# A transformer block on one core: a later x tile, other scale loads, a touch of the modulation rows, and other PSUM banks

## The chip, the cores and the metric

The kernel runs on one core of one Trainium2 chip. Its time is the device time of one execution in microseconds (us). It is given as the median over runs, and one further execution was taken with the hardware profiler. TensorE is called PE below, its weight loads PEld, VectorE DVE, ScalarE ACT, GpSimd POOL and SyncE SP.

## What is computed

This is a diffusion transformer block. A vector c gives six rows of modulation, two of which scale and shift the normalised x before attention; a third gates the attention's result; the other three do the same for the MLP. B = 2, N = 256, D = 1152, two heads of 576, F = 4608, all in bfloat16.

```python
mod = (_silu(c) @ w_mod).reshape(B, 6, 1, D)
shift_a, scale_a, gate_a, shift_m, scale_m, gate_m = [mod[:, i] for i in range(6)]
h = _layernorm(x, axis=-1) * (1 + scale_a) + shift_a
qkv = (h @ wqkv).reshape(B, N, 3, H, Dh)
...
attn = _softmax(jnp.einsum('bqhd,bkhd->bhqk', q, k) * Dh ** (-0.5), axis=-1)
a = jnp.einsum('bhqk,bkhd->bqhd', attn, v).reshape(B, N, D) @ wo
x = x + gate_a * a
h2 = _layernorm(x, axis=-1) * (1 + scale_m) + shift_m
m = _gelu(h2 @ w_fc1) @ w_fc2
return x + gate_m * m
```

## The kernel before

The 512 rows of x are four tiles of 128 (t = 0 to 3; tiles 0 and 1 are batch 0), and D is nine slices of 128 (kt = 0 to 8). All matrices stay in bfloat16; sums are in PSUM, eight banks of 512 float32 columns.

*Order.* A small planner (class `Sched`) records every operation as a unit with a cost and what it reads and writes, and derives the waits. PE and SP run their units in the order in which the program records them. DVE and ACT begin with lists written by hand (`S.first`); after these, and on POOL from the start, the planner takes the ready unit with the longest path behind it. Nearly all records carry a helper's line: every matmul is L693, every PE transpose L696, every DMA L674, PSUM copies on ACT L688 and on DVE L690.

*Head.* ACT's queue loads c, SP's queue loads x as two halves (`ld_x0`, `ld_x1`, two tiles each), then columns 0 to 639 of the scale matrix in three parts of three kt each (`ld_sc0_0`, `_3`, `_6`), then K's weights `ld_wk0` to `ld_wk4`, the other scale columns (`ld_sc5_*`), and so on. POOL makes the identity (`ones` L715, `ident` L716), which PE needs for everything. PE begins with filler matmuls of 512 columns on the identity (`warm_a`, then after the transpose of c, `c_T`, `warm_b` and so on). silu(c) is made by ACT and DVE (L729 to L731). Normalisation takes its sums on DVE for tiles 1 and 2 (`bn_stats`, L738) and on ACT for tiles 0 and 3 (L746, L747), POOL takes the root (`rstd`, L742 and L751), and DVE writes the normalised tile `xn_t` (L760). PE transposes it into PSUM (`xn_T(t)`), and 45 matmuls of two columns (`sca_kt`, `mod_kt`) give the scale for kt 0 to 4 in bank 7.

DVE adds 1 (`sc1a`, L799), and `hk(kt, b)` (L808 on DVE, L806 on ACT) multiplies the transposed slice in PSUM by it; `xn_T_copy` saves slices 5 to 8 in SBUF for later. Then K begins: `k_pair(kts, i, b)` adds slices kts to two of K's output tiles for batch b. For batch 0 it goes kt by kt over four pairs, with `xn_T(2)` after kt 1 and `xn_T(3)` after kt 2; then comes batch 1. In between, `scb` makes the scale for kt 5 to 8 as rows (36 matmuls, four in the array at a time), a DVE transpose (`scb_T`, L870) and an addition (L872) turn it into columns, and K goes on with kt 5.

*Middle and end.* Shift, Q, softmax, V and the attention's product follow. In `wo_tile(t)` PE makes three pieces of 384 columns, DVE multiplies each by the gate row (`wo_t1`, L1114), POOL adds x (L1115), and DVE and ACT normalise (L738, L1119, L1120). `xn2_T(t)` transposes the result into banks 7 and 6, from where DVE (L1135) and ACT (L1138) write the scaled and shifted slices. The accumulators of these pieces and of the MLP's tiles go around over six banks (`acc`). The first `F0` = 8 tiles of the MLP's first matrix are computed as two halves of 256 rows, the others over all 512. The second matrix (`fc2`) goes tile by tile in pieces of 384 columns; for each, DVE multiplies (L1232) and adds (L1233), and SP stores. The last piece is cut into 224, 96 and 64 columns.

Of the kernel before, what the change touches and what calls it, by code (L numbers as in the profile page):

```python
# [506 lines left out]
CH = 384  # L507
NCH = 3
F0 = 8
KC = 5  # L510
# [33 lines left out]
def build_kernel(nc, x, c, wqkv, wo, w_mod, w_fc1, w_fc2, out):  # L544
# [5 lines left out]
    with (  # L550
# [148 lines left out]
        dma(CSB[0:18, :], c.rearrange("b (k p) -> (b k) p", p=P), 18 * 256, "ld_c", eng="act")  # L699
        for b in range(2):  # L700
            dma(X[:, 2 * b:2 * b + 2, :], xv[b], 2 * P * D * 2, "ld_x%d" % b)
        for (ka, kb) in ((0, KC), (KC, KT)):
            w = (kb - ka) * P
            for k0 in range(0, KT, 3):
                dma(WSC[:, k0:k0 + 3, ka * P:kb * P], wmod_v[:, k0:k0 + 3, D + ka * P:D + kb * P], 3 * P * w * 2,
                    "ld_sc%d_%d" % (ka, k0), run=w * 2)
            for kt in range(ka, kb):
                dma(WK[:, kt, :], wqkv_v[:, kt, D:2 * D], P * D * 2, "ld_wk%d" % kt, run=2304)
        for k0 in range(0, KT, 3):
            dma(WSH[:, k0:k0 + 3, :], wmod_v[:, k0:k0 + 3, 0:D], 3 * P * D * 2, "ld_sh%d" % k0, run=2304)  # L710
# [8 lines left out]

        S.op("pool", 100, lambda e: e.memset(NHALF, -0.5), writes=[NHALF], name="nhalf")  # L720

        dve(600, lambda e: e.memset(Q4B, 0.0), [], [Q4B], "zq4b")
        for i in range(2):
            S.unit("pe", 430.0, "warm_a%d" % i)
            mm(ps32(5), IDENT, Q4B, True, True)
# [27 lines left out]
        for t in range(4):  # L753
            xt, xn, mv, rs = X[:, t, :], XN[:, t, :], MV[:, t, :], RSTD[:, t:t + 1]
            if t in (1, 2):
                ln_stats_dve(xt, [X[:, t, i * CH:(i + 1) * CH] for i in range(NCH)], BN[:, t, :], mv, rs, "ln1_%d" % t)
            else:
                ln_stats_act(xt, xn, mv, SUMS[:, t:t + 1], rs, "ln1_%d" % t)
            m = MV[:, t, 0:1]
            dve(c_dve_fast(D), lambda e, xt=xt, xn=xn, m=m, rs=rs: e.tensor_scalar(out=xn, in0=xt, scalar1=m, scalar2=rs,  # L760
                                                                                 op0=ALU.subtract, op1=ALU.mult),
                [xt, m, rs], [xn], "xn_%d" % t)


        XB = [(4, 5, 6), (6, 4, 5)]

        def xn_T(t):
            b = t // 2
            S.unit("pe", KT * c_mm(128), "xnT_%d" % t)
            for kt in range(KT):  # L770
                tr(ps16(XB[b][kt // 4], (kt % 4) * 256 + (t % 2) * 128, 128), XN[:, t, kt * 128:(kt + 1) * 128], IDENT)

        def xn_T_copy(b, k0, k1, eng):
            src = ps16(XB[b][k0 // 4], (k0 % 4) * 256, (k1 - k0) * 256).rearrange("p (k t) -> p k t", k=k1 - k0)
            copy_on(eng, HX[:, k0:k1, b * 256:(b + 1) * 256], src, (k1 - k0) * 256, True, "xnT_cp%d_%d" % (b, k0))
# [6 lines left out]
        def mod_kt(W, kt, col0, name, fs=(0, 9)):  # L782
            S.unit("pe", (fs[1] - fs[0]) * 27.0, name)
            for f in range(*fs):
                mm(ps32(7, col0 + f * 2, 2), W[:, kt, f * 128:(f + 1) * 128], ST[:, kt:18:9], kt == 0 and f == fs[0], kt == KT - 1,
                   skip_group_check=True)
# [10 lines left out]
        def sc1a(ka, kb):  # L797
            m, o = ps32(7, 2 * ka, 2 * (kb - ka)), SC1A[:, 2 * ka:2 * kb]
            dve(170, lambda e: e.tensor_scalar(out=o, in0=m, scalar1=1.0, scalar2=None, op0=ALU.add), [m], [o], "sc1a_%d" % ka)  # L799


        def hk(kt, b, eng="dve"):
            dst, s1 = HK[:, kt, b * 256:(b + 1) * 256], SC1A[:, kt * 2 + b:kt * 2 + b + 1]
            src = ps16(XB[b][kt // 4], (kt % 4) * 256, 256) if kt < KC else HX[:, kt, b * 256:(b + 1) * 256]
            if eng == "act":
                act(c_act(256, 1), lambda e: e.activation(out=dst, in_=src, func=ACTF.Copy, scale=s1), [src, s1], [dst], "hk_%d_%d" % (kt, b))  # L806
                return
            dve(256 if kt < KC else 200, lambda e: e.tensor_scalar(out=dst, in0=src, scalar1=s1, scalar2=None, op0=ALU.mult),  # L808
                [src, s1], [dst], "hk_%d_%d" % (kt, b))
# [7 lines left out]
        KB = [(0, 1, 2, 3), (5, 4, 6)]  # L817
# [18 lines left out]
        warm(15, "b")  # L836
        xn_T(1)
        for kt in range(0, 3):
            mod_kt(WSC, kt, 0, "sca_%d" % kt, (0, KC))
        warm(1, "c")  # L840
        xn_T(0)
        for kt in range(3, 6):
            mod_kt(WSC, kt, 0, "sca_%d" % kt, (0, KC))
        warm(2, "d")
        for kt in range(6, 9):
            mod_kt(WSC, kt, 0, "sca_%d" % kt, (0, KC))
        warm(3, "e")
        sc1a(0, KC)
        for kt in range(KC):
            hk(kt, 0, "act" if kt in (2, 4) else "dve")  # L850
        xn_T_copy(0, 8, 9, "act")
        xn_T_copy(0, 5, 8, "act")
        for kt in range(KC):
            for i in range(4):
                k_pair((kt,), i, 0)
            if kt == 1:
                xn_T(2)
            if kt == 2:
                xn_T(3)
                xn_T_copy(1, 8, 9, "act")  # L860
                xn_T_copy(1, 5, 8, "act")
        for kt in range(KC):
            hk(kt, 1, "act" if kt == 2 else "dve")
        k_pair(range(KC), 0, 1)
        S.unit("pe", KT * 4 * 27.0, "scb")
        for kt in range(KT):
            quad_mm(6, WSC[:, kt, :], KC, KT, kt)
        n = 32 * (KT - KC)
        sct, scr = ps32(6, 0, n), MT[:, 0:n]
# [6 lines left out]
        k_pair(range(KC), 1, 1)  # L876
        k_pair(range(KC), 2, 1)
# [34 lines left out]
        for kt in range(KT):  # L912
            for b in range(2):
# [5 lines left out]
                else:  # L919
# [174 lines left out]
        acc = [2, 3, 4, 5, 0, 1]  # L1094
# [29 lines left out]
        def xn2_T(t):  # L1124
# [3 lines left out]
            slot = [ps16(7, kt * 128, 128) if kt < 4 else ps16(6, (kt - 4) * 128, 128) for kt in range(KT)]  # L1128
# [161 lines left out]
```

## Time and profile before

| | |
|---|---|
| median of 3 runs | 245.28 us (244.84 to 245.52) |
| profiled execution: time, span | 245.29 us, 243.5 us |
| PE busy | 238.5 us (98%) in 1721 instructions |
| DVE, ACT, POOL busy | 117.0, 67.0, 22.4 us |
| DMA | 51.57 MB, 212 GB/s over the span, some 390 GB/s up to about 70 us |
| granted TensorE clock | 0.999 |

The span runs from the first to the last instruction of the profiled execution; its time has 1.8 us more around it. In a line of the timeline stand the start, the time from the first to the last of the merged instructions, engine, line, operation, output and input, the count, and in brackets how long the engine had been idle before it and what ended that. A matmul's record covers its way through the array, so matmuls overlap, and their pace is read from one start to the next. "DMA to landing" runs from an issue to the last of its 16 completions.

### The profile page before, as it was taken

Reading aid. Unit: us, or ns where it says so; the run is one execution under the profiler, and the core shown is the slowest. Engines: PE = TensorE matmul, PEld = TensorE weight load, DVE = VectorE, ACT = ScalarE, POOL = GpSimd, SP = SyncE. Lnnn points to the kernel's source line nnn. Section 1 sums busy time; section 2 is a strip of 40 time slices with the busy share of each in tenths; the row PEclk is TensorE's granted clock in tenths of the full one; section 3 lists DMA queues with packets and bytes.
Section 4 is the critical chain, followed back from the end, with each engine's and each line's share of the span. In section 5 each row is a group of like instructions: output and inputs, shape, how many; then the busy total and the mean of one; then the engine's idle time right before and its main releaser. Section 6 shows DMA issues by size and latency. Waiting matters only on the chain.

```text
span 243.5 us, 4013 instructions
## 1 busy us (share of the span) xinstructions
PE 238.5 (98%) x1721; PEld 145.9 (60%) x1731; DVE 117.0 (48%) x227; ACT 67.0 (27%) x137; POOL 22.4 (9%) x40
## 2 busy tenths in 40 slices
PE   7999999999999999999999999999999999999995
PEld 2587844466667666888444444444565656566675
DVE  3644359798892689779999500000022221111112
ACT  5630340435614206973223332222000000000000
POOL 1400000000023275500000110000000000000000
PEclk9999999999999999999999999999999999999999
DMA  6999999999995999979943499100000000000000
GB/s 240 361 377 392 391 385 388 405 415 404 387 340 156 351 389 392 391 239 397 338 145 87 167 271 398 57 0 3 0 16 19 16 16 16 19 16 17 31 19 16
DMA packets 30139, 51.57 MB, mean 212 GB/s; under 512 B 1707, under 2 KB 16939, under 8 KB 30123
## 3 DMA queue, kind: packets, MB, share of 16 engines
q1 hardware_dynamic: 29584, 50.14, 57.5%
q0 software_dynamic: 512, 1.19, 1.6%
q8 instruction: 13, 0.21, 0.4%
q14 instruction: 3, 0.02, 0.0%
q10 hardware_dynamic: 27, 0.00, 0.0%
HBM read 50.14 MB, written 1.19 MB: 211 GB/s over the span
## 4 chain that ended last, share of the span: by engine, by line
PE 97%; ACT 1%; issue 0%; DVE 0%; POOL 0%; POOLq 0%
PE psum L693 94%; PE psum L696 2%; ACT arena L1138 1%; ACT arena L1120 1%; DVE arena L808 0%; POOL arena L716 0%; DVE arena L1232 0%; DVE arena L1233 0%; POOL arena L715 0%; DVE arena L799 0%; POOL arena L1022 0%; POOL arena L720 0%; POOLq L1275 0%
## 5 line engine op out<-in xcount | busy, mean ns | idle before, releaser
L693 PE MATMUL psum<-arena 128*128 128x384 bf16 (+9 forms) x1632 | 235.3, 312 | 2.3 <-POOL arena L716 1.5
L693 PEld LDWEIGHTS psum<-arena 128*128 128x128 bf16 (+1 forms) x1642 | 140.5, 97 | 92.5 <-issue 5.2
L1232 DVE TENSOR_TENSOR arena<-psum,arena 128x384 f32<-128x384 f32 (+3 forms) x14 | 7.0, 500 | 89.4 <-PE psum L693 89.4
L1148 ACT ACTIVATE arena<-psum 128x512 bf16<-128x512 f32 (+1 forms) x44 | 22.5, 522 | 42.6 <-PE psum L693 42.6
L688 ACT ACTIVATE arena<-psum 128x512 bf16<-128x512 f32 (+6 forms) x37 | 18.9, 539 | 37.9 <-PE psum L693 37.9
L1049 DVE SCALAR_TENSOR_TENSOR arena<-arena 128x1152 f32<-128x1152 bf16 x16 | 21.3, 1409 | 0.0
L1020 DVE SCALAR_TENSOR_TENSOR arena<-arena 128x896 f32<-128x896 bf16 x16 | 17.6, 1145 | 0.0
L690 DVE CAST arena<-psum 128x512 bf16<-128x512 f32 (+1 forms) x12 | 7.7, 646 | 12.1 <-PE psum L693 12.0
L674 POOL DMA_DIRECT2D dit_scratch<-arena x6 | 3.6, 605 | 95.7 <-ACT arena L688 58.1
L1115 POOL TENSOR_TENSOR arena<-arena 128x384 f32<-128x384 f32 x12 | 10.9, 912 | 11.3 <-DVE arena L1114 10.2
L738 DVE BATCH_NORM_STATS2 arena<-arena 128x6 f32<-128x384 f32 (+1 forms) x18 | 9.5, 549 | 1.5 <-DMA arena<-in_x_dram 0.9
L1120 ACT ACTIVATE arena<-arena 128x1152 bf16<-128x1152 f32 x4 | 5.4, 1353 | 9.5 <-DVE arena L1119 9.5
L1114 DVE TENSOR_TENSOR arena<-psum,arena 128x384 f32<-128x384 f32 x12 | 6.5, 546 | 2.7 <-PE psum L693 1.3
L696 PEld LDWEIGHTS psum<-arena 128*128 128x128 bf16 (+1 forms) x89 | 6.0, 98 | 2.4 <-DMA arena<-in_c_dram 0.8
L696 PE MATMUL psum<-arena 128*128 128x128 bf16 (+1 forms) x89 | 7.3, 219 | 0.1
L1233 DVE TENSOR_TENSOR arena<-arena 128x384 bf16<-128x384 f32 (+3 forms) x14 | 7.0, 502 | 0.5
L1138 ACT ACTIVATE arena<-psum,arena 128x128 bf16<-128x128 bf16 x16 | 6.1, 459 | 3.2 <-PE psum L696 2.5
L1135 DVE TENSOR_SCALAR arena<-psum,arena 128x128 bf16<-128x128 bf16 x20 | 5.5, 336 | 1.9 <-PE psum L696 1.8
L808 DVE TENSOR_SCALAR arena<-psum,arena 128x256 bf16<-128x256 bf16 x7 | 2.4, 349 | 3.6 <-PE psum L696 2.3
L742 POOL TENSOR_TENSOR arena<-arena 128x1 f32<-128x1 f32 x6 | 3.3, 553 | 5.9 <-DVE arena L741 5.9
L964 ACT ACTIVATE arena<-psum,arena 128x256 bf16<-128x256 f32 x8 | 3.7, 470 | 0.0
L917 ACT ACTIVATE arena<-arena 128x256 bf16<-128x256 bf16 x6 | 2.5, 495 | 3.3 <-DVE arena L911 3.3
(57 smaller groups left out, 53.2 us busy)
## 6 DMA issues: line engine op xcount, KB each, us to landing
arena<-in_w_fc_dram SPq DMA_DIRECT2D x9, 1152.0 KB, 7.2
arena<-in_w_fc_dram SPq DMA_DIRECT2D x4, 2592.0 KB, 18.0
arena<-in_w_mod_dram SPq DMA_DIRECT2D x3, 1920.0 KB, 20.4
arena<-in_wqkv_dram SPq DMA_DIRECT2D x18, 288.0 KB, 9.7
arena<-in_w_mod_dram SPq DMA_DIRECT2D x3, 864.0 KB, 12.4
arena<-in_wqkv_dram SPq DMA_DIRECT2D x1, 2592.0 KB, 16.1
arena<-in_wo_dram SPq DMA_DIRECT2D x1, 2592.0 KB, 26.2
arena<-in_w_mod_dram SPq DMA_DIRECT2D x1, 2592.0 KB, 17.9
```

Of the source, the lines that this page charges most:

```text
L688: act(c_act(n), lambda e: e.activation(out=dst, in_=src, func=ACTF.Copy), [src], [dst], name)
L690: dve(c_dve_psum16(n) if psum16 else c_dve_psum32(n), lambda e: e.tensor_copy(dst, src), [src], [dst], name)
L693: S.instr(lambda e: e.matmul(o, lhsT=l, rhs=r, start=st, stop=sp, **kw), reads=[l, r], writes=[o])
L696: S.instr(lambda e: e.transpose(o, i_, idn), reads=[i_, idn], writes=[o])
L738: dve(550, lambda e, s=s, o=o: e.bn_stats(out=o, in_=s), [s], [o], "bn_%s_%d" % (tag, ci))
L1020: dve(150 + FG * 1.1, lambda e, o=o, w=w, s1=s1: e.scalar_tensor_tensor(out=o, in0=w, scalar=s1, in1=o, op0=ALU.mult, op1=ALU.add), [w, s1 ...
L1049: u = dve(1300, lambda e, o=o, w=w, s1=s1: e.scalar_tensor_tensor(out=o, in0=w, scalar=s1, in1=o, op0=ALU.mult, op1=ALU.add), [w, s1, o], ...
L1115: S.op("pool", 930, lambda e, xs=xs, x1c=x1c: e.tensor_tensor(out=x1c, in0=x1c, in1=xs, op=ALU.add), reads=[x1c, xs], writes=[x1c], name=" ...
L1120: act(1344, lambda e: e.activation(out=xn2, in_=x1, func=ACTF.Identity, scale=rs, bias=nm), [x1, rs, nm], [xn2], "xn2_%d" % t)
L1138: act(440, lambda e, o=o, dst=dst, s1=s1, s2=s2: e.activation(out=dst, in_=o, func=ACTF.Identity, scale=s1, bias=s2), [o, s1, s2], [dst], ...
L1148: act(c_act(ntok), lambda e: e.activation(out=dst, in_=o, func=ACTF.Gelu_apprx_tanh), [o], [dst], "gelu_%d_%d" % (f, tok0))
L1232: dve(c_dve_psum32(w), lambda e, o=o, gm=gm, t1=t1: e.tensor_tensor(out=t1, in0=o, in1=gm, op=ALU.mult), [o, gm], [t1], "fc2_t1_%d_%d" % ( ...
```

## The change

- Loads: ACT's queue begins with a read of 64 bytes from every ninth row of w_mod (128 rows) into space that is used only later (`touch`), and c moves to POOL's queue. x comes as tiles 0 and 1 together, then tile 2, and tile 3 only after `ld_wk1`. The first scale columns come in parts of 2, 3, 3 and 1 kt.
- PE's head: five `warm_a` and ten `warm_b` fillers instead of two and fifteen; two scale slices before `xn_T(1)`, three between it and `xn_T(0)`, four after it, and two fillers then. A scale matmul streams 64 columns (silu(c) repeated 32 times) instead of 2, into 64 columns of bank 7, of which `sc1a` reads two.
- Normalisation: tile 2 takes its sums on ACT, tile 3 on DVE. The first slice of batch 0 is copied to SBUF before it is scaled.
- K: `xn_T(3)` comes after the first two pairs of kt 4, batch 1's slices lie in the banks by odd and even kt, batch 1 adds them in the order 0, 2, 1, 4, 3, its second pair comes ahead of `scb` instead of after it, and `scb` goes to bank 7.
- Later: four accumulator banks until the second halves of the MLP's first tiles and six after; `xn2_T` of odd t in banks 1 and 0; F0 = 9; the last piece in 304 and 80 columns.

```diff
@@ -506,7 +506,7 @@
 NCH = 3
-F0 = 8
+F0 = 9
 KC = 5
...
@@ -696,16 +696,18 @@
-        dma(CSB[0:18, :], c.rearrange("b (k p) -> (b k) p", p=P), 18 * 256, "ld_c", eng="act")
-        for b in range(2):
-            dma(X[:, 2 * b:2 * b + 2, :], xv[b], 2 * P * D * 2, "ld_x%d" % b)
-        for (ka, kb) in ((0, KC), (KC, KT)):
+        dma(sb(O_PT, 64), w_mod.rearrange("(p k) f -> p k f", k=KT)[:, 0, D:D + 32], P * 64, "touch", eng="act")
+        dma(X[:, 0:2, :], xv[0], 2 * P * D * 2, "ld_x0")
+        dma(X[:, 2, :], xv[1][:, 0, :], P * D * 2, "ld_x2", run=2304)
+        for (ka, kb, cuts) in ((0, KC, (0, 2, 5, 8, 9)), (KC, KT, (0, 3, 6, 9))):
             w = (kb - ka) * P
-            for k0 in range(0, KT, 3):
-                dma(WSC[:, k0:k0 + 3, ka * P:kb * P], wmod_v[:, k0:k0 + 3, D + ka * P:D + kb * P], 3 * P * w * 2,
+            for k0, k1 in zip(cuts, cuts[1:]):
+                dma(WSC[:, k0:k1, ka * P:kb * P], wmod_v[:, k0:k1, D + ka * P:D + kb * P], (k1 - k0) * P * w * 2,
                     "ld_sc%d_%d" % (ka, k0), run=w * 2)
...
                 dma(WK[:, kt, :], wqkv_v[:, kt, D:2 * D], P * D * 2, "ld_wk%d" % kt, run=2304)
+                if kt == 1:
+                    dma(X[:, 3, :], xv[1][:, 1, :], P * D * 2, "ld_x3", run=2304)
         for k0 in range(0, KT, 3):
...
@@ -717,12 +719,13 @@
+        dma(CSB[0:18, :], c.rearrange("b (k p) -> (b k) p", p=P), 18 * 256, "ld_c", eng="pool")
         S.op("pool", 100, lambda e: e.memset(NHALF, -0.5), writes=[NHALF], name="nhalf")
...
         dve(600, lambda e: e.memset(Q4B, 0.0), [], [Q4B], "zq4b")
-        for i in range(2):
+        for i in range(5):
             S.unit("pe", 430.0, "warm_a%d" % i)
-            mm(ps32(5), IDENT, Q4B, True, True)
+            mm(ps32(7), IDENT, Q4B, True, True)
         CT_PS = ps16(7, 0, 18)
...
@@ -752,7 +755,7 @@
             xt, xn, mv, rs = X[:, t, :], XN[:, t, :], MV[:, t, :], RSTD[:, t:t + 1]
-            if t in (1, 2):
+            if t % 2 == 1:
                 ln_stats_dve(xt, [X[:, t, i * CH:(i + 1) * CH] for i in range(NCH)], BN[:, t, :], mv, rs, "ln1_%d" % t)
...
@@ -762,17 +765,24 @@
-        XB = [(4, 5, 6), (6, 4, 5)]
+        def xt_ps(b, kt, n=1):
+            if b == 0:
+                return (4, 5, 6)[kt // 4], (kt % 4) * 256
+            return (5, 0) if kt == 8 else ((6, 4)[kt % 2], kt // 2 * 256)
...
             for kt in range(KT):
-                tr(ps16(XB[b][kt // 4], (kt % 4) * 256 + (t % 2) * 128, 128), XN[:, t, kt * 128:(kt + 1) * 128], IDENT)
-
-        def xn_T_copy(b, k0, k1, eng):
-            src = ps16(XB[b][k0 // 4], (k0 % 4) * 256, (k1 - k0) * 256).rearrange("p (k t) -> p k t", k=k1 - k0)
-            copy_on(eng, HX[:, k0:k1, b * 256:(b + 1) * 256], src, (k1 - k0) * 256, True, "xnT_cp%d_%d" % (b, k0))
+                bank, c0 = xt_ps(b, kt)
+                tr(ps16(bank, c0 + (t % 2) * 128, 128), XN[:, t, kt * 128:(kt + 1) * 128], IDENT)
+
+        def xn_T_copy(b, kts, eng):
+            bank, c0 = xt_ps(b, kts[0])
+            n = len(kts)
+            src = ps16(bank, c0, n * 256).rearrange("p (k t) -> p k t", k=n)
+            st = kts[1] - kts[0] if n > 1 else 1
+            copy_on(eng, HX[:, kts[0]:kts[-1] + 1:st, b * 256:(b + 1) * 256], src, n * 256, True, "xnT_cp%d_%d" % (b, kts[0]))
...
@@ -781,8 +791,9 @@
             S.unit("pe", (fs[1] - fs[0]) * 27.0, name)
+            sv = ST[:, kt:18:9].unsqueeze(1).broadcast_to([P, 32, 2])
             for f in range(*fs):
-                mm(ps32(7, col0 + f * 2, 2), W[:, kt, f * 128:(f + 1) * 128], ST[:, kt:18:9], kt == 0 and f == fs[0], kt == KT - 1,
+                mm(ps32(7, f * 64, 64).rearrange("p (n b) -> p n b", b=2), W[:, kt, f * 128:(f + 1) * 128], sv, kt == 0 and f == fs[0], kt == KT - 1,
                    skip_group_check=True)
...
@@ -795,13 +806,15 @@
         def sc1a(ka, kb):
-            m, o = ps32(7, 2 * ka, 2 * (kb - ka)), SC1A[:, 2 * ka:2 * kb]
+            m = ps32(7, 64 * ka, 64 * (kb - ka)).rearrange("p (f n) -> p f n", n=64)[:, :, 0:2]
+            o = SC1A.rearrange("p (k b) -> p k b", b=2)[:, ka:kb, :]
             dve(170, lambda e: e.tensor_scalar(out=o, in0=m, scalar1=1.0, scalar2=None, op0=ALU.add), [m], [o], "sc1a_%d" % ka)
...
             dst, s1 = HK[:, kt, b * 256:(b + 1) * 256], SC1A[:, kt * 2 + b:kt * 2 + b + 1]
-            src = ps16(XB[b][kt // 4], (kt % 4) * 256, 256) if kt < KC else HX[:, kt, b * 256:(b + 1) * 256]
+            bank, c0 = xt_ps(b, kt)
+            src = ps16(bank, c0, 256) if kt < KC and kt + b > 0 else HX[:, kt, b * 256:(b + 1) * 256]
             if eng == "act":
...
@@ -814,7 +827,7 @@
-        KB = [(0, 1, 2, 3), (5, 4, 6)]
+        KB = [(0, 1, 2, 3), (5, 6, 4)]
         ev_rr = [0]
...
@@ -833,48 +846,49 @@
-        warm(15, "b")
+        warm(10, "b")
+        for kt in range(0, 2):
+            mod_kt(WSC, kt, 0, "sca_%d" % kt, (0, KC))
         xn_T(1)
-        for kt in range(0, 3):
+        for kt in range(2, 5):
             mod_kt(WSC, kt, 0, "sca_%d" % kt, (0, KC))
-        warm(1, "c")
         xn_T(0)
-        for kt in range(3, 6):
+        for kt in range(5, 9):
             mod_kt(WSC, kt, 0, "sca_%d" % kt, (0, KC))
-        warm(2, "d")
-        for kt in range(6, 9):
-            mod_kt(WSC, kt, 0, "sca_%d" % kt, (0, KC))
-        warm(3, "e")
+        warm(2, "e")
+        xn_T_copy(0, (0,), "dve")
         sc1a(0, KC)
         for kt in range(KC):
-            hk(kt, 0, "act" if kt in (2, 4) else "dve")
-        xn_T_copy(0, 8, 9, "act")
-        xn_T_copy(0, 5, 8, "act")
+            hk(kt, 0, "act" if kt == 4 else "dve")
+        xn_T_copy(0, (8,), "act")
+        xn_T_copy(0, (5, 6, 7), "act")
         for kt in range(KC):
-            for i in range(4):
+            for i in range(2 if kt == KC - 1 else 4):
                 k_pair((kt,), i, 0)
...
                 xn_T(2)
-            if kt == 2:
-                xn_T(3)
-                xn_T_copy(1, 8, 9, "act")
-                xn_T_copy(1, 5, 8, "act")
+        xn_T(3)
+        k_pair((KC - 1,), 2, 0)
+        k_pair((KC - 1,), 3, 0)
+        xn_T_copy(1, (8,), "act")
+        xn_T_copy(1, (5, 7), "act")
+        xn_T_copy(1, (6,), "dve")
         for kt in range(KC):
-            hk(kt, 1, "act" if kt == 2 else "dve")
-        k_pair(range(KC), 0, 1)
+            hk(kt, 1, "act" if kt % 2 else "dve")
+        k_pair((0, 2, 1, 4, 3), 0, 1)
+        k_pair((0, 2, 1, 4, 3), 1, 1)
         S.unit("pe", KT * 4 * 27.0, "scb")
         for kt in range(KT):
-            quad_mm(6, WSC[:, kt, :], KC, KT, kt)
+            quad_mm(7, WSC[:, kt, :], KC, KT, kt)
         n = 32 * (KT - KC)
-        sct, scr = ps32(6, 0, n), MT[:, 0:n]
+        sct, scr = ps32(7, 0, n), MT[:, 0:n]
         dve(c_dve_psum32(n), lambda e: e.transpose(scr, sct), [sct], [scr], "scb_T")
...
                 hk(kt, b)
-        k_pair(range(KC), 1, 1)
-        k_pair(range(KC), 2, 1)
+        k_pair((0, 2, 1, 4, 3), 2, 1)
         for kt in range(KT):
...
@@ -924,11 +938,11 @@
         S.first = {
-            "dve": ["zq4b", "c_half", "c_silu", "bn_ln1_1_0", "bn_ln1_1_1", "bn_ln1_1_2", "aggr_ln1_1", "veps_ln1_1", "bn_ln1_2_0", "nvar_ln1_0", "veps_ln1_0",
-                    "xn_1", "xn_0", "bn_ln1_2_1", "bn_ln1_2_2", "aggr_ln1_2", "veps_ln1_2", "nvar_ln1_3", "veps_ln1_3",
-                    "sc1a_0", "hk_0_0", "xn_2", "hk_1_0", "xn_3", "hk_3_0", "hk_0_1", "hk_1_1", "hk_3_1", "hk_4_1", "scb_T", "sc1a_5"],
-            "act": ["ld_c", "c_tanh", "sq_ln1_0", "sum_ln1_0", "sq_ln1_3", "sum_ln1_3", "xnT_cp0_8", "xnT_cp0_5", "hk_2_0", "hk_4_0",
-                    "hk_2_1", "xnT_cp1_8", "xnT_cp1_5"],
+            "dve": ["zq4b", "c_half", "c_silu", "bn_ln1_1_0", "bn_ln1_1_1", "bn_ln1_1_2", "aggr_ln1_1", "veps_ln1_1", "nvar_ln1_0", "veps_ln1_0",
+                    "xn_1", "xn_0", "nvar_ln1_2", "veps_ln1_2", "xnT_cp0_0", "sc1a_0", "hk_0_0", "hk_1_0", "hk_2_0", "hk_3_0", "xn_2",
+                    "bn_ln1_3_0", "bn_ln1_3_1", "bn_ln1_3_2", "aggr_ln1_3", "veps_ln1_3", "xn_3", "hk_0_1", "hk_2_1", "hk_4_1", "xnT_cp1_6", "scb_T", "sc1a_5"],
+            "act": ["touch", "c_tanh", "sq_ln1_0", "sum_ln1_0", "sq_ln1_2", "sum_ln1_2", "xnT_cp0_8", "xnT_cp0_5", "hk_4_0",
+                    "xnT_cp1_8", "hk_1_1", "hk_3_1", "xnT_cp1_5"],
         }
...
@@ -1091,7 +1105,7 @@
-        acc = [2, 3, 4, 5, 0, 1]
+        acc = [2, 3, 4, 5]
         acc_rr = [0]
...
@@ -1125,7 +1139,8 @@
             S.unit("pe", KT * c_mm(128), "xn2T_%d" % t)
-            slot = [ps16(7, kt * 128, 128) if kt < 4 else ps16(6, (kt - 4) * 128, 128) for kt in range(KT)]
+            hi, lo = ((7, 6), (1, 0))[t % 2]
+            slot = [ps16(hi, kt * 128, 128) if kt < 4 else ps16(lo, (kt - 4) * 128, 128) for kt in range(KT)]
             for kt in range(KT):
...
@@ -1206,6 +1221,9 @@
         mlp_gate(last_h2T[0])
+        k = acc_rr[0] % 4
+        acc[:] = [0, 1] + acc[k:] + acc[:k]
+        acc_rr[0] = 0
         for f in range(F0):
...
@@ -1220,7 +1238,7 @@
             if t == 3:
-                pieces = [(0, CH), (CH, 2 * CH), (2 * CH, 3 * CH - 160), (3 * CH - 160, 3 * CH - 64), (3 * CH - 64, 3 * CH)]
+                pieces = [(0, CH), (CH, 2 * CH), (2 * CH, 3 * CH - 80), (3 * CH - 80, 3 * CH)]
             for (c0, c1) in pieces:
...
```

## The prediction

> **What bounds the kernel now.** I read the busy times and the chain of waits first.
>
> ```profile
> PE 238.5 (98%) x1721; PEld 145.9 (60%) x1731; DVE 117.0 (48%) x227; ACT 67.0 (27%) x137; POOL 22.4 (9%) x40
> ...
> PE 97%; ACT 1%; issue 0%; DVE 0%; POOL 0%; POOLq 0%
> ```
>
> TensorE (PE) is busy for 238.5 of 243.5 us and carries 97% of the chain. So the time is PE's work plus PE's holes, and a change pays only if K's first matmul starts sooner, a hole closes, or the tail shrinks. Then the timeline of the first 13 us.
>
> ```profile
> 1.15 0.28 POOL L716 TENSOR_SCALAR_AFFINE_SELECT arena<-arena 128x128 bf16<-128x128 bf16 x1
> ...
> 1.49 1.03 PE L693 MATMUL psum<-arena 128*128 128x512 bf16 x2 [1.49 <-POOL arena L716]
> ...
> 2.45 0.10 PEld L696 LDWEIGHTS psum<-arena 18*128 18x128 bf16 x1 [0.84 <-DMA arena<-in_c_dram]
> ...
> 6.82 0.15 PEld L693 LDWEIGHTS psum<-arena 128*128 128x128 bf16 x1 [0.27 <-issue]
> ...
> 7.25 0.15 PEld L693 LDWEIGHTS psum<-arena 128*128 128x128 bf16 x1 [0.28 <-issue]
> ...
> 7.66 0.31 PEld L693 LDWEIGHTS psum<-arena 128*128 128x128 bf16 x2 [0.26 <-issue]
> ...
> 8.21 0.58 DVE L760 TENSOR_SCALAR arena<-arena 128x1152 bf16<-128x1152 bf16 x1 [0.45 <-POOL arena L751]
> ...
> 9.42 0.67 PE L696 MATMUL psum<-arena 128*128 128x128 bf16 x9
> ...
> 10.95 0.72 PEld L693 LDWEIGHTS psum<-arena 128*128 128x128 bf16 x18 [0.54 <-DMA arena<-in_w_mod_dram]
> 11.65 0.17 DVE L799 TENSOR_SCALAR arena<-psum 128x10 f32<-128x10 f32 x1 [1.16 <-PE psum L693]
> 11.86 0.35 DVE L808 TENSOR_SCALAR arena<-psum,arena 128x256 bf16<-128x256 bf16 x1
> ...
> 12.26 0.77 PEld L693 LDWEIGHTS psum<-arena 128*128 128x128 bf16 x8 [0.59 <-DVE arena L808]
> ```
>
> PE starts at 1.49, when ident (L716) ends. Its filler matmuls start 0.43 us apart (6.82, 7.25) until the weight loads of 7.66, and 0.215 apart after: half clock, then full. Tile 0 is normalised by 8.79 (8.21 + 0.58), the last transposes of batch 0 run at 9.42, and PE then waits for a scale load that lands at 10.9 (the DMA view: issued at 2.7, 8.2 us to landing). 15 scale matmuls later come sc1a (11.65), hk_0_0 (11.86), and K at 12.27. From there PE has no hole over 0.33 us. The next one that matters lies around scb:
>
> ```profile
> 19.02 1.59 PEld L693 LDWEIGHTS psum<-arena 128*2 128x2 bf16 x46 [0.21 <-issue]
> ...
> 20.48 0.32 DVE L870 STREAM_TRANSPOSE arena<-psum 128x128 f32<-128x128 f32 x1 [1.83 <-PE psum L693]
> 20.83 0.17 DVE L872 TENSOR_SCALAR arena<-arena 128x8 f32<-128x8 f32 x1
> 20.85 0.66 PEld L693 LDWEIGHTS psum<-arena 128*128 128x128 bf16 x7 [0.23 <-DVE arena L870]
> 21.04 0.68 DVE L808 TENSOR_SCALAR arena<-arena 128x256 bf16<-128x256 bf16 x3
> ```
>
> scb runs from 19.02 and PE goes on at 19.63, but its transpose on VectorE (DVE) starts only at 20.48, 1.45 us after scb's start: 36 matmuls issued in 0.46 us report about 33 ns apart. The stage that needs the result (K of kt 5) starts at 21.95, when k_pair(2,1) is through (20.85 + 10 x 0.109). One hole is left at xn2_T(1), 0.25 us until ACT frees the bank:
>
> ```profile
> 97.43 0.28 PEld L696 LDWEIGHTS psum<-arena 128*128 128x128 bf16 x5 [0.26 <-ACT arena L1138]
> ```
>
> **The change part by part.** The sum goes against the profiled execution, 245.29 us (span 243.5, 1.8 around it); the median of the runs is 245.28.
>
> *Loads.* x3 (288 KB) goes behind wk1. Landings near it come 0.75 us apart for 288 KB (wk0 11.71, wk1 12.45), so the last scale part lands at 10.9 - 0.75 = 10.15, wk0 at 10.95, and x3 where wk1 was, about 12.4. The last scale part is one tile, so 5 matmuls and not 15 follow it. One more SP issue (0.45 us) is nothing: the queue runs 5 us ahead. The touch adds 128 packets of 64 bytes, 8 per DMA engine. Read one by one, 46 of the 1152 first scale packets were slow (up to 594 ns where 55 is normal; 6.6 us in all, 0.4 per engine). The touch can at best take these 0.4 us out of the scale loads, and at worst puts them and its own packets before x0: -0.4 to +0.5 on the landings. I take 0, because the same accesses are only moved.
>
> *c on GpSimd (POOL).* The planner has ld_c ready at time 0 with a longer path behind it than nhalf, and ident not yet, so POOL issues it between ones and ident. A POOL issue takes 0.605 us (first one 0.78). It thus starts at about 0.95, ident ends at about 1.95, and PE starts at 2.0 instead of 1.49. Five warm_a at 0.427 then run until 4.13, and there c_T stands in PE's order with everything behind it. The nearest rows for the landing are the small POOL stores:
>
> ```profile
>
> ```
>
> One by one: 1.7 us with idle engines, 2.4, 2.0 and 3.2 later, but 5.8 and 5.2 for the first two, under a full SP queue. So c lands between 2.65 and 6.75; I take at most 4.1, as four of six rows do, and keep the other end for a rival. [...]
>
> *PE up to K.* c_T ends at 4.25. Ten warm_b: eight at half clock to 7.67, two at 0.215, to 8.1. The 64-column scale matmuls cost 29 ns each (the 64-column piece of fc2 starts one every 29.2 ns) against 26 ns for two columns: +0.13 us over 45, of which under 0.1 counts. sca_0, 1: 0.29; xn_T(1) 0.51; sca_2 to 4: 0.44; xn_T(0) 0.51, at 9.34 (tile 0 is ready at 8.8, so a later x0 has 0.45 us of cover); sca_5 to 8: 0.58. That ends at 10.43, with the last load in at 10.15. Before, K came 0.90 after the last scale matmul; now hk_0_0 reads SBUF (282 ns, L808) and not PSUM (349), so 0.80 after the last start at 10.40: **K starts at 11.2, 1.07 us sooner.**
>
> *What is late next.* xn_T(3) needs x3, and DVE takes it only after hk_0 to hk_3 and xn_2: bn_3 from 12.5 (x3 is in at 12.4), three of them 1.48, aggr and veps 0.46, rstd 0.65, xn_3 0.6, so xn_T(3) at 15.75. PE comes there at 11.2 + 16 x 0.109 + 0.51 + 20 x 0.109 = 15.65, a hole of 0.1. Then 0.5 of transposes and 0.44 of pairs, to 16.7; but hk_0_1 starts only when the transposes are done (16.45), so k_pair(0,1) starts at 16.85, another 0.15. With hk split over DVE and ACT it and k_pair(1,1) run to 19.1, and scb starts at 19.2 (its last load landed at 18.76). Now only one k_pair (1.09) covers scb's return: PE is free at 20.9, and 1.45 + 0.35 + 0.21 + 0.3 after scb's start hk_5_0 is done, 21.5. **A hole of 0.6 that before did not have; K of kt 5 starts at 21.5 against 21.95: 0.45 of the 1.07 is left.**
>
> *Later.* xn2_T(1) gets banks 1 and 0: -0.25. Its rows follow PE (t1_2_1 on DVE at 92.28 waits for PE), so its input moves along; if not, the gain is 0. xn2_T(3)'s 0.05 hole goes too. Four accumulators instead of six: wo_1_1 now waits for the multiply of wo_0_0, which waits for the gate row until 82.95 and ends at 83.5; PE comes at about 85.7, so 2.2 us of cover, after which each missing us costs one. F0 = 9: 18 x 0.109 instead of 9 x 0.216, +0.02. The last tile's pieces of 304 + 80 columns replace 224 + 96 + 64: 36 x (95.8 + 42.5 + 29.2) = 6.03 us becomes 36 x (129 + 36) = 5.94, less 0.04 for two wider DVE steps: -0.05.
>
> Sum: -0.45 - 0.25 - 0.05 + 0.02 - 0.05 = -0.78: 245.29 - 0.78 = **244.5**. Own range 244.0 to 245.0: 0.3 either way from K's start, 0.25 from xn2_T(1).
>
> **Rivals.**
> *c comes late (slower).* For it: the first POOL store of the run took 5.8 us from issue to landing, and c's would be the first and stand beside the same full SP queue. Against it: that store's first packet moved only after 2.9 us, while the later small ones moved after 1.1. With c at 6.4, ten cold warm_b end at 10.8, K starts 2.7 later than above at 13.9, x3's hole of 0.1 is swallowed: 244.5 + 2.6 = 247.1. It decides from a landing 0.8 us past the cover, 4.9; between 4.1 and 4.9 it is no change.
> *The clock steps later (no change).* If the step to full clock follows PE's start (6.2 us after it, from this trace) it comes at 8.2: two warm_b more at 0.427, +0.42, 244.9. [...]
> *The start is quicker than I sum it (faster).* If POOL's issue does not hold ident (PE from 1.5) or the clock steps sooner, PE reaches xn_T(0) at 8.9, when tile 0 is ready, 0.45 sooner; if the touch also takes the 0.4 us out of the scale loads, these follow. hk_0 to 3, xn_2 and bn_3 move along: 244.0. For it: engines 0.6 to 0.7 busy from 1.5 to 2.5, room for the touch. Against it: 605 ns rows that follow one another without overlap.
> *The touch does nothing.* Then landings are as summed, and so is the time.
>
> **How the numbers follow.** About 0.3% (0.74 us) is what a measurement tells from no change: faster is below 244.5, slower above 246.0. The forecast has 0.55 and sits on that edge: 0.30 faster, 0.25 same. Quick start 0.17: faster. Later clock 0.09: same, 0.02 of it slower. c late 0.19: 0.16 slower, 0.03 same. Faster 0.47, same 0.35, slower 0.18. The range 243.8 to 246.3 holds the first three and those landings of c that cost under 1.8 us; above it lies about 0.13, below it 0.05.
>
> **What would show it.** Right: c_T near 4.2, K near 11.2, scale landing near 10.1, a hole of about 0.6 ahead of K of kt 5 with PE waiting for hk_5_0, none at xn2_T(1). Wrong: PE waiting for in_c past 4.9; fillers 0.43 apart past 8.2; K before 10.8; x0 landing later than 4.8; PE waiting for wo's multiply on its third and fourth bank.

## The result and the profile after

The changed kernel takes 247.72 us (median; 247.14 to 247.87) against 245.28: a ratio of 1.0099 (95% interval 1.0087 to 1.011), slower by 1%. The forecast was 244.5 with a range to 246.3: other sign, and outside the range. The profiled execution took 247.14 us, the quickest of the five; its span was 245.4.

In a few executions of four of the experiments (1 to 3 of 12) the granted clock was 0.993 on average and the time 1 to 2 us longer; their medians and ratios include these. A ratio below compares with executions of the kernel before that were taken beside the experiment; their medians were 245.15 to 245.39, so medians of different experiments compare to about 0.2 us.

The page of the changed kernel, busy times and chain:

```profile
PE 238.1 (97%) x1689; PEld 146.5 (60%) x1698; DVE 116.6 (48%) x227; ACT 67.1 (27%) x138; POOL 22.9 (9%) x41
...
PE 96%; DMA 2%; DVE 1%; issue 1%; POOL 0%; POOLq 0%
```

PE is as busy as before to 0.4 us and the span is 1.9 us longer. New in the chain are the 2% of DMA. Its timeline up to K:

```profile
1.33 0.66 POOL L674 DMA_DIRECT2D arena<-in_c_dram  x1 [0.33 <-issue]
...
2.08 0.32 POOL L718 TENSOR_SCALAR_AFFINE_SELECT arena<-arena 128x128 bf16<-128x128 bf16 x1
...
2.45 2.31 PE L693 MATMUL psum<-arena 128*128 128x512 bf16 x5 [2.45 <-POOL arena L723]
...
5.79 0.19 PE L696 MATMUL psum<-arena 18*128 18x18 bf16 x1 [1.03 <-DMA arena<-in_c_dram]
...
5.91 4.29 PE L693 MATMUL psum<-arena 128*128 128x512 bf16 x20
...
8.80 1.22 PEld L693 LDWEIGHTS psum<-arena 128*128 128x128 bf16 x12 [0.20 <-issue]
...
9.24 1.23 DVE L763 TENSOR_SCALAR arena<-arena 128x1152 bf16<-128x1152 bf16 x2 [0.17 <-POOL arena L745]
...
10.54 1.05 PE L693 MATMUL psum<-arena 128*128 128x64 bf16 x15
...
11.93 1.76 PE L693 MATMUL psum<-arena 128*128 128x64 bf16 x21
...
13.30 0.17 DVE L811 TENSOR_SCALAR arena<-psum 128x10 f32<-128x10 f32 x1 [0.88 <-PE psum L693]
...
13.84 1.21 PEld L693 LDWEIGHTS psum<-arena 128*128 128x128 bf16 x12 [0.65 <-DVE arena L821]
```

c is issued at 1.33 and lands at 5.74; five fillers are through by then, and PE stands still until c_T at 5.79. From there PE works without a hole to the last scale matmul, so everything behind c_T is late by what c_T is late. The 15 scale matmuls take from 10.54 to 11.37, 59 ns from start to start. K starts at 13.84: 1.58 later than before, where 1.07 sooner was forecast. At scb:

```profile
21.79 1.59 PEld L693 LDWEIGHTS psum<-arena 128*2 128x2 bf16 x46 [0.21 <-issue]
...
23.25 0.32 DVE L885 STREAM_TRANSPOSE arena<-psum 128x128 f32<-128x128 f32 x1 [3.19 <-PE psum L693]
...
24.14 1.42 PEld L693 LDWEIGHTS psum<-arena 128*128 128x128 bf16 x14 [0.76 <-DVE arena L821]
```

PE has nothing left to cover scb's return and waits 0.65 us ahead of K of kt 5, at 24.15 (before 21.95: 2.20 later). After that xn2_T(1) and (3) run without their holes (1.94 later at the MLP), and a new one comes:

```profile
109.92 1.16 ACT L1153 ACTIVATE arena<-psum,arena 128x128 bf16<-128x128 bf16 x3 [0.82 <-PE psum L693]
...
111.19 0.89 PEld L693 LDWEIGHTS psum<-arena 128*128 128x128 bf16 x9 [0.32 <-DVE arena L1150]
```

At the second half of the MLP's first tile PE waits 0.235 us (2.14 later). The profile names DVE, but DVE wrote its last slice at 110.82 (109.22 + 1.60); PE's next weight load starts 0.11 after ACT's last slice (109.92 + 1.16 = 111.08). The last tile gives 0.09 back on PE, another 0.17 lies between PE's last matmul and the end (2.65 us instead of 2.81), and the span is 1.9 longer.

### The profile page after: what moved, and what is told of

It is laid out like the page before. It is cut to its first block, busy times and chain, and to the rows that moved or that the text cites. A ratio compares the mean times of both kernels' runs of the same rounds, so it can differ in the third digit from the quotient of the medians.

```text
span 245.4 us, 3949 instructions
## 1 busy us (share of the span) xinstructions
PE 238.1 (97%) x1689; PEld 146.5 (60%) x1698; DVE 116.6 (48%) x227; ACT 67.1 (27%) x138; POOL 22.9 (9%) x41
## 4 chain that ended last, share of the span: by engine, by line
PE 96%; DMA 2%; DVE 1%; issue 1%; POOL 0%; POOLq 0%
PE psum L693 94%; PE psum L696 2%; DMA arena<-in_c_dram 2%; DVE arena L821 0%; DVE arena L885 0%; DVE arena L1250 0%; DVE arena L1251 0%; POOL arena L717 0%; DVE arena L887 0%; DVE arena L811 0%; POOLq L1293 0%
## 5 line engine op out<-in xcount | busy, mean ns | idle before, releaser
L693 PE MATMUL psum<-arena 128*128 128x384 bf16 (+8 forms) x1600 | 235.0, 315 | 3.9 <-POOL arena L723 2.4
L693 PEld LDWEIGHTS psum<-arena 128*128 128x128 bf16 (+2 forms) x1609 | 141.2, 97 | 93.4 <-issue 4.6
L1250 DVE TENSOR_TENSOR arena<-psum,arena 128x384 f32<-128x384 f32 (+2 forms) x13 | 6.8, 526 | 88.8 <-PE psum L693 88.8
L696 PEld LDWEIGHTS psum<-arena 128*128 128x128 bf16 (+1 forms) x89 | 5.9, 98 | 2.9 <-DMA arena<-in_c_dram 1.9
L1251 DVE TENSOR_TENSOR arena<-arena 128x384 bf16<-128x384 f32 (+2 forms) x13 | 6.8, 527 | 0.4
L974 DVE TENSOR_REDUCE arena<-psum 128x2 f32<-128x512 f32 x4 | 2.7, 686 | 1.0 <-PE psum L693 1.0
```

Of the source, the lines that this page charges most:

```text
L693: S.instr(lambda e: e.matmul(o, lhsT=l, rhs=r, start=st, stop=sp, **kw), reads=[l, r], writes=[o])
L696: S.instr(lambda e: e.transpose(o, i_, idn), reads=[i_, idn], writes=[o])
L1250: dve(c_dve_psum32(w), lambda e, o=o, gm=gm, t1=t1: e.tensor_tensor(out=t1, in0=o, in1=gm, op=ALU.mult), [o, gm], [t1], "fc2_t1_%d_%d" % ( ...
L1251: dve(c_dve_32(w), lambda e, t1=t1, x1c=x1c, ost=ost: e.tensor_tensor(out=ost, in0=t1, in1=x1c, op=ALU.add), [t1, x1c], [ost], "fc2_out_%d ...
```

## The experiments

Three causes were open: c's late landing, the 59 ns, and the new holes. Landings and single starts below are read one by one from the traces.

**c back on ScalarE's queue.**

```diff
-dma(sb(O_PT, 64), ..., "touch", eng="act")
+dma(CSB[0:18, :], ..., "ld_c", eng="act")
+dma(sb(O_PT, 64), ..., "touch", eng="act")
...
-dma(CSB[0:18, :], ..., "ld_c", eng="pool")
```

> The changed kernel with c back at the head of ScalarE's queue and the touch behind it. Theory C (the late c is the whole loss: it held PE, ScalarE and VectorE until 5.8 us): K starts near 11.2 instead of 13.84, 245.1 us. Theory W (besides, the 64-column scale matmuls start 59 ns apart and not 29, so 45 of them hold the path longer by 1.3 us): c lands at 2.3, tile 0 is normalised near 9.3, K starts near 12.4, about 246.2 us, still slower than before.

```profile
0.79 0.58 ACTq L674 DMA_DIRECT2D arena<-in_c_dram  x1
...
1.49 2.31 PE L693 MATMUL psum<-arena 128*128 128x512 bf16 x5 [1.49 <-POOL arena L719]
...
3.73 0.19 PE L696 MATMUL psum<-arena 18*128 18x18 bf16 x1
```

245.51 us, ratio to before 1.0017 (1.0007 to 1.0028): 2.21 less than with c on GpSimd, although the touch is now issued at 1.41 instead of 0.80. c lands at 2.19, c_T runs at 3.73 behind its five fillers, K starts at 12.13. c's place is most of the loss.

**Two columns instead of 64, c left on GpSimd.**

```diff
-mm(ps32(7, f * 64, 64)..., W[...], sv, ...)
+mm(ps32(7, col0 + f * 2, 2), W[...], ST[:, kt:18:9], ...)
```

> The changed kernel with two-column scale matmuls as before; c stays on GpSimd's queue. Theory C alone: the matmuls had time while everything waited for c, K near 13.8, 247.7 us. Theory W: xn_T(0) still waits for tile 0 (10.5), the twenty matmuls behind it take 0.55 instead of 1.2 us and those ahead of it are hidden: K near 12.5, about 246.3 us.

246.41 us, ratio 1.0053 (1.0039 to 1.0067): 1.31 less than the changed kernel, so the columns cost far more than the forecast's 0.1.

**Both** (the two diffs above).

> Both undone: c on ScalarE's queue ahead of the touch, two-column scale matmuls. Theories C and W together: K near 11.2 us as the prediction had it; the hole of 0.65 us ahead of K of kt 5 stays; 245.0 us. If K stays at 12 or later, a third cause holds the start (x0, 0.5 us later behind the touch, or the last scale load).

244.94 us, ratio 1.0008 (0.999 to 1.0026), not to be told from before; two of the twelve executions, 246.65 and 246.82, pull the ratio up. The profiled execution, at full clock, took 244.60. The steps 247.72, 245.51, 244.94 put about 2.2 us on c's queue and, with c early, about 0.6 on the columns; with c late the columns cost 1.31. It fits that with c late nothing but PE's own work stands between c_T and K, while with c early part of it hides behind the scale loads (PE's weight loads wait 0.37 us for one at 9.80). K starts at 11.22 here, where the forecast had 11.2, but at 11.46, 11.51 and 11.80 in three other profiles with the same head.

**Before, with c alone moved to GpSimd.**

```diff
-dma(CSB[0:18, :], ..., "ld_c", eng="act")      # ahead of x
+dma(CSB[0:18, :], ..., "ld_c", eng="pool")     # ahead of nhalf
```

> The kernel before with only c moved to GpSimd's queue. Theory C: c lands near 5.7 us, VectorE and ScalarE start the normalisation near 6.2 instead of 4.3, PE runs its 15 fillers behind c, xn_T(1) near 10.5 instead of 8.3: K near 14, 247.0 us. Rival (the late c costs only where the wide matmuls follow it): K below 12.8, under 245.8 us.

248.28 us, ratio 1.0127 (1.0114 to 1.014). c lands at 5.88; PE has only two fillers ahead of c_T and stands idle 2.2 us. K starts at 15.02, 2.75 later than before. The same edit costs more in the kernel before.

**Silu behind the statistics on ScalarE and VectorE.** In the changed kernel these two also wait for c: ScalarE's first sum starts at 6.09 and VectorE's first statistics at 6.62, though x0 landed at 4.78. Is that what delays K?

```diff
-"dve": ["zq4b", "c_half", "c_silu", "bn_ln1_1_0", ..., "veps_ln1_1", "nvar_ln1_0", ...
+"dve": ["zq4b", "bn_ln1_1_0", ..., "veps_ln1_1", "c_half", "c_silu", "nvar_ln1_0", ...
-"act": ["touch", "c_tanh", "sq_ln1_0", "sum_ln1_0", ...
+"act": ["touch", "sq_ln1_0", "c_tanh", "sum_ln1_0", ...
```

> The change as it is (c on GpSimd's queue, 64 columns), only that ScalarE takes sq of tile 0 ahead of c_tanh, and VectorE the statistics of tile 1 ahead of c_half and c_silu, so that neither waits for c. Theory P (c's lateness acts through PE's own order: fillers, transposes and scale matmuls follow c_T without a hole): tile 0 is normalised about 1 us sooner (9.5 against 10.47), and K still starts at 13.8; time 247.7. Theory Q (it acts through the two engines that wait for silu first): K starts about 1 us sooner, time 246.7.

```profile
4.66 1.48 DVE L741 BATCH_NORM_STATS2 arena<-arena 128x6 f32<-128x384 bf16 x3 [3.46 <-DMA arena<-in_x_dram]
...
8.57 0.58 DVE L763 TENSOR_SCALAR arena<-arena 128x1152 bf16<-128x1152 bf16 x1 [0.44 <-POOL arena L754]
...
14.06 0.17 DVE L811 TENSOR_SCALAR arena<-psum 128x10 f32<-128x10 f32 x1 [0.88 <-PE psum L693]
```

Tile 0 is normalised at 9.15 instead of 10.47, and nothing is won: 247.7 us, ratio 1.0085 (1.0064 to 1.0106). (sc1a comes even later in this execution, because all ten fillers behind c_T ran at half clock, some 0.43 us apart.) c's lateness acts through PE's order.

**c second on ScalarE's queue, behind the touch.** Is it GpSimd that is slow, or is c late behind x?

```diff
 dma(sb(O_PT, 64), ..., "touch", eng="act")
+dma(CSB[0:18, :], ..., "ld_c", eng="act")
-dma(CSB[0:18, :], ..., "ld_c", eng="pool")
```

> The change with c on ScalarE's queue, but second, behind the touch (64 columns as in the change). Theory G (a GpSimd DMA is slow by itself under a full SP queue): c, issued at about 1.2 us by ScalarE, lands by 3.2, PE starts at 1.49, time 245.3 to 245.8. Theory X (what is issued after x's first load, on whatever queue, moves only when that load's packets are nearly through: the touch behind c on ScalarE's queue was issued at 1.41 and its first packet moved at 4.3, as c's on GpSimd's queue, issued at 1.33, moved at 4.45): c's first packet moves after 3.5 us, c lands at about 5, PE stands idle for about 1.3 us behind its five fillers, time 247.0 to 247.5.

```profile
1.23 0.60 ACTq L674 DMA_DIRECT2D arena<-in_c_dram  x1
...
1.49 2.32 PE L693 MATMUL psum<-arena 128*128 128x512 bf16 x5 [1.49 <-POOL arena L719]
...
5.07 0.19 PE L696 MATMUL psum<-arena 18*128 18x18 bf16 x1 [1.26 <-DMA arena<-in_c_dram]
```

246.76 us, ratio 1.0067 (1.0042 to 1.0092), a little below what theory X gave and far from G. c's first packet moves at 3.77, 2.5 us after its issue, when x0's packets are nearly through (the last starts at 3.99); first in the same queue it moved 0.95 us after its issue. This run alone leaves a rival: the touch's packets stand ahead of c in the same queue, and move from 2.04 to 4.16. Two others speak for x's packets. In the experiment with c back on ScalarE's queue the touch, issued at 1.41 behind c, whose packets had all started by 1.85, first moved at 4.32. And in the kernel before with c on GpSimd, which has no touch, c first moved at 4.82, while the last packet of x started at 5.11. So most of the lateness is not GpSimd's. The rest, 247.72 - 246.76 or about 1 us, goes with c_T at 5.79 instead of 5.07, by a landing 0.72 later; with four executions between 246.4 and 247.5 its size is rough.

**What the 64 columns cost.** Four layouts of the moving operand in one kernel; the scale of kt 2 to 7 isn't the reference's.

```diff
+if W is WSC and kt in (2, 5):   # one element, 64 times
+    sv, ov = ST[:, 0:1].broadcast_to([P, 64]), ...
+if W is WSC and kt in (3, 6):   # 64 neighbours
+    sv, ov = Q4B[:, 0:64], ...
+if W is WSC and kt in (4, 7):   # two neighbours, 32 times
+    sv = Q4B[:, 0:2].unsqueeze(1).broadcast_to([P, 32, 2])
```

> A look at the pace of the 64-column scale matmuls, with c first on ScalarE's queue. The moving operand is silu(c) repeated as in the change (two elements nine apart, 32 times) for kt 0, 1 and 8; one element 64 times for kt 2 and 5; 64 neighbouring elements for kt 3 and 6; two neighbouring elements 32 times for kt 4 and 7. For kt 2 to 7 the scale is therefore not that of the reference, and the time isn't to be read. Theory S (59 ns is the price of the operand's layout): the 64 neighbouring elements start 29 ns apart like fc2's 64-column piece, the change's form 59 apart; whether repetition or distance makes it, the two other forms tell. Theory N (59 ns is the price of 64 columns in this place, whatever the layout): all four forms start 59 ns apart.

Theory S. Starts read one by one from the trace at full clock, five matmuls of each kt:

```
two elements nine apart, 32 times (kt 8)    59 ns
two neighbours, 32 times (kt 4)             31 ns
one element, 64 times (kt 2)                31 to 34 ns
64 neighbours (kt 3)                        28 to 29 ns
```

Repetition was nearly free here (31 to 34 ns against 28 to 29); the distance is what cost (59 against 31). silu(c) lies with the two batches nine elements, 18 bytes, apart. Why the distance costs is not shown; none between 2 and 18 bytes was tried.

**Without the touch** (c first, two columns).

```diff
-dma(sb(O_PT, 64), ..., "touch", eng="act")
```

> The change with c first on ScalarE's queue, two-column scale matmuls, and without the touch. Theory T (the touch takes slow accesses off the scale loads): without it the last scale part lands about 0.4 us later than 10.2, K starts at about 11.6, time 245.3 against 244.9 with the touch. Theory H (the touch's 128 packets stand before x and the scale loads and only cost): x0 lands at 4.25 and not at 4.35, the last scale part at about 10.0, K at 11.0, time 244.7. Theory N (it does nothing): landings as before to 0.1 us, time 244.9. From the runs so far N is likeliest: 5.11 us pass from the landing of x's third tile to that of the last scale part with the touch, 5.24 us before the change for the same bytes.

The last scale part lands at 10.89, K starts at 11.91, 245.16 us, ratio 0.9989 (0.9972 to 1.0005): the landing is nearer to theory T, and the time can't be told from the version with the touch. But x's third tile landed later too (5.43 against 5.10), and the 5.46 us from there to the last scale part are no more than the 5.1 to 5.6 with the touch behind c. The other runs say more. From x's last landing ahead of the scale loads to the last of these it takes 4.3 to 4.9 us in the four kernels that issue the touch at 0.8 on ScalarE's queue (changed, two columns, silu late, c second), 5.1 to 5.6 in the six that issue it at 1.41 behind c, and 5.2 to 5.5 in the three without it (before, before with c on GpSimd, and this one). So it shortens the loads if its packets go ahead, by some 0.7 us, and x0 then lands at 4.6 to 4.8 instead of 4.2 to 4.6. In those four kernels c is late as well; the last version below has the touch ahead with c early.

**k_pair(1,1) behind scb again** (c first, two columns).

```diff
-k_pair((0, 2, 1, 4, 3), 1, 1)      # ahead of scb
...
+k_pair((0, 2, 1, 4, 3), 1, 1)      # behind scb
 k_pair((0, 2, 1, 4, 3), 2, 1)
```

> The change with c first on ScalarE's queue, two-column scale matmuls, and k_pair(1,1) behind scb again as before the change. Theory R (the hole of 0.56 to 0.65 us ahead of K of kt 5 is scb's return over VectorE, which one k_pair doesn't cover): the hole goes, K of kt 5 starts about 0.5 us sooner, time 244.4 against 244.9. Theory L (the hole is the late landing of the last part of the second scale columns, 18.2 to 19.9 us in the runs so far, and scb standing earlier in PE's order only waits for it): PE waits ahead of or inside scb at about 18.1, K of kt 5 starts at the same time or later, time 244.9 to 245.4.

245.05 us, ratio 0.9989 (0.9972 to 1.0005). The hole ahead of K of kt 5 is gone, as theory R has it, but no gain in time shows: 244.94 with the pair ahead of scb, and theory R gave 244.4. The profiled execution (246.1) shows something else; windows of it, in the columns PE, PEld, DVE, ACT, POOL, granted clock, DMA:

```profile
8.90:12.30 3.40, 2.75 (x51) 2.00 (x52) 1.81 (x9) 2.18 (x5) 0.55 (x1) 0.98 1.04 396
12.30:15.70 3.40, 3.40 (x23) 2.66 (x21) 2.63 (x8) 0.00 (x0) 0.55 (x1) 0.51 1.07 375
15.70:17.00 1.30, 1.30 (x16) 1.18 (x14) 0.53 (x1) 0.00 (x0) 0.00 (x0) 1.00 1.13 356
```

PE's clock fell to half from 12.29 to 15.72, and K's matmuls started 0.213 us apart instead of 0.109.

**Banks 0 and 1 last among the accumulators** (c first, two columns).

```diff
-acc[:] = [0, 1] + acc[k:] + acc[:k]
+acc[:] = acc[k:] + acc[:k] + [0, 1]
```

> The change with c first on ScalarE's queue and two-column scale matmuls, and with banks 0 and 1 last instead of first in the order of the six accumulators. Theory B (the hole of 0.23 us at the second half of the MLP's first tile is bank 0, in which the last transposed slices of tile 3 still wait to be read by ScalarE): the hole goes, time 0.2 us less, 244.7 against 244.9. Rival (PE waits for the slices themselves, because F0 = 9 puts the transposes of tile 3 one tile of the MLP later): the hole stays, 244.9.

244.89 us, ratio 0.9979 (0.9963 to 0.9995). The hole is gone: 49 matmuls run on without one while ACT still reads tile 3's slices.

```profile
106.70 5.51 PE L693 MATMUL psum<-arena 128*128 128x256 bf16 x49
...
107.61 1.16 ACT L1151 ACTIVATE arena<-psum,arena 128x128 bf16<-128x128 bf16 x3 [0.82 <-PE psum L693]
```

Theory B: PE waited for bank 0. The medians (244.89 and 244.94) differ by less than 0.2; they can't show so little, since K's start alone differs by more between executions (11.22 to 11.80 in the four profiles with the same head).

**The four edits together, and the touch on SP.** The first version has the four edits above (c first, two columns, the pair, the banks), of which the last two showed as closed holes and not in a time of their own; the second differs from it in the touch's queue:

```diff
-dma(sb(O_PT, 64), ..., "touch", eng="act")     # behind c
+dma(sb(O_PT, 64), ..., "touch")                # on SP, ahead of x0
```

> A version meant to be faster than both: c first on ScalarE's queue, two-column scale matmuls, k_pair(1,1) behind scb, banks 0 and 1 last among the accumulators. The two holes of 0.6 and 0.23 us are gone: 244.9 - 0.55 - 0.23 = 244.1 if the landings are as in the run with c first and two columns; up to 244.7 if the scale loads land 0.6 us later, as they did in three of the five runs in which the touch was issued behind c.

**244.37 us** (244.09 to 244.68), ratio 0.996 (0.9945 to 0.9976): faster than both kernels. The last scale part lands at 10.46 (10.21 to 10.79 in the earlier runs with the touch behind c). K starts at 11.50 and kt 5 9.97 later (10.37 with the pair ahead of scb). Not all of the hole of 0.65 is won, because scb now comes before its last load, as theory L of the pair's experiment had it:

```profile
18.41 0.32 PEld L693 LDWEIGHTS psum<-arena 128*2 128x2 bf16 x24 [0.21 <-issue]
19.01 3.99 PEld L693 LDWEIGHTS psum<-arena 128*2 128x2 bf16 x47 [0.28 <-DMA arena<-in_w_mod_dram]
```

> The same version with the touch first on SP's queue instead of behind c on ScalarE's. Theory E (the touch shortens the scale loads only if its packets move before theirs: last scale part at 9.8 to 10.0 us in three runs in which it was issued at 0.8, at 10.2 to 10.8 in four in which it was issued at 1.41 and its packets stood beside x's last, 10.9 in one without it): x0 lands 0.4 us later at 4.8, the last scale part at 9.9 or sooner, K starts at 11.0 to 11.2, time 243.9. Theory M (the difference comes from c's queue or from chance): the last scale part lands 0.4 us later than with the touch behind c, K at 11.6, time 244.5.

244.59 us, ratio 0.9972 (0.9961 to 0.9983). The scale loads are as short as theory E says (4.5 us behind x's), but x0 lands 0.7 later than in the version above, at 5.27, and so the last scale part lands no sooner (10.49, before it 10.46). K starts at 11.79: theory M's time by another road. The slow accesses moved into x0's packets: summed over its 128 packets, the excess over the usual 178 ns is 10.6 us, 4.2 in the version above, while that of the scale loads over their usual 55 ns falls from 8.4 to 4.2.

## Why the prediction was wrong

**c's landing: the step that failed.** The forecast took at most 4.1 for the landing, as four of six small GpSimd stores did. These are their groups in the DMA view of before (output and input, count, KB each, median from issue to landing):

```profile
dit_scratch<-arena POOLq DMA_DIRECT2D x3, 0.5 KB, 5.2
...
dit_scratch<-arena POOLq DMA_DIRECT2D x2, 1.8 KB, 2.2
...
dit_scratch<-arena POOLq DMA_DIRECT2D x1, 4.0 KB, 1.7
```

c's landing was 5.74, 4.41 us after the issue. The other two rows (5.8 and 5.2 us), which stood under a full SP queue as c does, were the nearest ones, and they were kept for the rival at 0.19. The count of rows decided where the likeness of the situation should have. The runs name this step: with c early and the 64 columns kept the time is 245.51, inside the stated range; with c late and two columns it is 246.41, outside. What no row of before could tell: a small load behind x's first load was late on ScalarE's queue too (the touch behind c: 2.9 us from issue to first packet).

**The rival's numbers.** The rival's mechanism came true, at a price of 2.21 us. That its figures came so close (K at 13.9, time 247.1) is luck. In the changed kernel's profile K starts 2.65 later than summed: 1.66 is the end of c_T (5.91 instead of 4.25), 1.29 the scale matmuls, and the fillers give 0.31 back. Against the rival, c landed 0.66 sooner (5.74 instead of 6.4) and the fillers took about 0.7 less, and the 1.29 us of columns, which the rival didn't have, made up for both.

**PE's start.** Forecast 2.0, measured 2.45: the issue began at 1.33, not 0.95, and ident ran behind it. PE had to wait for c anyway, so the late start itself cost nothing here.

**The 64 columns: a mis-sized term.** 29 ns each came from fc2's piece, whose operand lies in one row; 59 was measured. Against 26 for two columns that is 45 x 0.033 = 1.5 us; about 1.3 of it showed with c late and 0.6 with c early, where 0.1 was put.

**The clock.** The likeliest case had the step at 7.67. With one and the same start (1.49) it came at 4.5 (c on ScalarE) and 7.2 (the fastest version), so it does not follow PE's start by 6.2 us. When PE stood idle for c it came at 8.1 (c second), 8.8 (changed), 10.2 (before with c on GpSimd), or behind all fillers (two columns, silu late). Of the fillers behind c_T seven to ten then ran at half clock (some 0.43 us apart, 0.215 at full), but with c early it was two to nine: where the step falls differs from execution to execution.

**The loads.** The last scale part was forecast at 10.15, landed at 9.84, and did not count. The range of the touch held; against the zero taken for it the scale part came 0.3 sooner and x0 0.5 later, to no effect on the sign.

**What held.** From K's start to kt 5 the forecast lost 0.62 (1.07 less 0.45); measured 10.30 against 9.69, 0.61, with a hole of 0.65 in the place named. x3 came in time (12.54; with K late this was no test, but with both undone it landed at 12.47 and PE had no hole there either); hk_0_1's hole was 0.29 instead of 0.15; xn2_T(1) gave its 0.25; four accumulators cost nothing at wo; the tail gave 0.25 instead of 0.05, 0.09 of it on PE and the rest behind PE's last matmul.

**What was missed.** Bank 0 first after tile 3's transposes into bank 0: 0.235 us. The new order of banks was costed at wo only, not where the order changes again.

**What the rest of the sum is worth.** With c on time and two columns, one profiled execution comes close to the forecast of -0.78: 244.60 - 245.29 = -0.69. Part of that is luck: bank 0 took 0.235 that was not in the sum, the tail gave 0.20 more than was in it, and K started earlier than in the three other profiles with the same head. Over twelve executions the same version can't be told from before (ratio 1.0008), so the parts behind K held, and the gain of the whole isn't shown.

## What to carry to other kernels

Issue a small load that the first engine in line waits for ahead of the large ones; here a small load issued some 0.5 us behind x's first one first moved 2.5 to 3.5 us after its issue, on ScalarE's queue and on GpSimd's. Where the profile has several rows for an unknown, take the one whose surroundings are the same, not the majority. Before a matmul's width is costed, look at how its moving operand lies: elements 18 bytes apart streamed at half the pace of neighbours (59 against 31 ns for 64 columns). And when accumulators change banks, ask at every change of order who still reads the bank that comes first.

## What was not expected of the hardware

- The pace of a 64-column matmul: 59 ns with elements 18 bytes apart, 31 with one pair of neighbours repeated.
- PE's clock fell back in the middle of a kernel that hardly pauses. In the pair's experiment it rose at 5.46, fell at 12.29 and rose at 15.72: 6.83 and 3.43 us apart. In the 3.40 us ahead of the fall PE was busy for 2.75, with no single gap over 0.35 us. What lowers the clock is not shown: in the same stretch of the fastest version PE was busy for 2.87 us, and there the clock stayed at 1.00. Seven of the 48 executions of four kernels fell, none of the 52 of the kernel before taken beside them. Why other executions with gaps as long kept their clock stays open. The kernel before has fillers between its scale matmuls where the changed one has gaps.
